# Splitting chains into single steps and ordering all steps anew, in a scan with a feed-forward block

## The chip, the cores and the metric

The kernel runs on one core of a Trainium2 chip. The metric is the device time of one execution in microseconds; the shown time is the median of three executions. A core has TensorE (PE in the profile, with its weight loads as PEld), VectorE (DVE), ScalarE (ACT), GpSimd (POOL) and SyncE (SP), whose queue issues the transfers of this kernel.

## The reference

Two blocks follow each other. The first is a scan with a state (4 batches, 8 heads, 768 tokens, head size 32, state size 16), the second a normalised feed-forward layer with a gate (3072 tokens, 256 features, 1536 hidden features), all in float32:

```python
log_a = np.log(np.clip(a, 1e-06, 1.0))
# per chunk of tokens, per batch and head:
cum = np.cumsum(la, axis=-1)
L = np.exp(cum[:, :, :, None] - cum[:, :, None, :]) * causal
y_intra = (C B^T * L) x
y_inter = C state * exp(cum)
state = exp(sum(la)) * state + sum_j B_j x_j exp(cum_last - cum_j)
# then, on (tokens, heads * head size):
xn = x / np.sqrt(np.mean(x * x, axis=-1, keepdims=True) + 1e-06) * rms_g
g = xn @ w_gate
out = (g * sigmoid(g) * (xn @ w_val)) @ w_out
```

The three weights arrive as 64-bit words and are turned into float32 on the chip.

## The kernel before

The 3072 tokens are worked through in six blocks of 512. A block has two pairs; a pair is two chunks of 128 tokens, in each of which the scan is computed in the two halves of 64. Per block the steps are:

- the scan: sums of logarithms and their exponentials `L` (ScalarE), products `g` of B and C (TensorE), their product with `L` (VectorE, L637 to L655), added states `A` (TensorE) and the running states `S` (VectorE, `states`, L685), the outputs `y` (TensorE, L709 and L740);
- the norm: `y` copied out into `yt` (`taken_out`, L805) and squared into `sq` (`squares`, L783), means by a product `ms` (L826), their root `rs` on ScalarE (`norm_roots`, L838), sent to memory and back, spread over the partitions, as `rb` (L849), then `xn` (L856);
- the gate and the value: for a pair of feature blocks `j`, seven products `P.1.j` to `P.7.j` of Strassen's scheme (`product_gv`, L947) in place of eight. A `take` copies a partial sum out of PSUM (ScalarE, L969), a `C` adds it to another (VectorE, L974), `silu` and `hid` follow;
- the output: twenty products `O.k` in two halves each (`product_o`, L1074) in place of twenty-seven, on sums of hidden values made by `u` and `up` (VectorE and GpSimd, L1058) and of weights. Totals `w.n` (`total_o`, L1097) bring them together on VectorE and ScalarE; `put` stores 128 rows. The product 1 uses the same part of PSUM as the product 11, so `O.1.0` waits until `w.18`, the total that reads product 11, has read it.

Block 0 starts before the weights are there. Its feature blocks 0 to 5 are made by plain products (`early.f.s` on values that are not yet normed, L883, and `gate.f`, L874), the other six by Strassen's scheme, and its output by a plain `o.f` (L996).

The startup goes like this. GpSimd builds masks: `never`, `after`, `hmask`, `upto` (L289, L298). VectorE casts `never` to `whole16`, and the steps `mask.p.h` write it with a product to the PSUM of a decay (L471). `idle.7` is seven products on zeros with no reader (L339). `a` is transposed (`aT`, L344), its logarithm `la0` taken, and products sum it: `r.0` (L400), `d`, `c` (L424 to L440). `parts.0` splits the sums in three 16-bit parts by four dependent operations on VectorE (L406), `turn` and `T` transpose B and C (L549, L565), `sums.p.h` (L478) adds the sums into the decays and `exp.p.h` (L500) takes the exponential.

A piece `k` of the weights goes through `fetch.k` (SyncE), `pow.k` (`power`, L217: three dependent operations on ScalarE), `man.k` (`mantissa`, L231: two on VectorE) and `wt.k` (L240: one on VectorE that joins both).

What sets the order: the kernel is built under a manual schedule, so every engine and SyncE's queue run their instructions in the order in which the program issues them. That order is a string `order` of 1667 steps (L1283), which a loop runs through (L1451). A step such as `0:gg.3/2` is the block, the kind, its numbers and the PSUM slot that it takes; `*2` behind a step puts two filler products into its bank first. The dictionaries `first_kinds` (L1199, block 0) and `kinds` (L1256) give the function for each kind. PSUM of block 0 has three slots of two banks (`/0`, `/1`, `/2`), given back by `switch.0` and `switch.1` to the tiles of the later blocks.

Of the kernel before, what the change touches and what calls it, by code (L numbers as in the profile page):

```python
# [10 lines left out]
I32 = mybir.dt.int32  # L11
# [9 lines left out]
def kernel(  # L21
# [195 lines left out]
    def power(k):  # L217
        words16, (lo, hi), dst, shape = fetched[k]
        n = shape[1] * shape[2]
        e = cvt.tile([P, n], FP32, tag="e", name="e", bufs=4)  # L220
# [6 lines left out]
        activation(out=b16, in_=g, func=AF.Prelu, scale=-2.0 ** 27, bias=kinks[:, 2:3],  # L227
                             alpha=2.0 ** -20)
        parts[k, "e"] = b16.bitcast(BF16)

    def mantissa(k):  # L231
        words16, (lo, hi), dst, shape = fetched[k]
        m = cvt.tile(shape, I32, tag="m", name="m")
        nc.vector.tensor_scalar(out=m, in0=hi, scalar1=0xFFFFF, scalar2=0x100000,  # L234
                                op0=ALU.bitwise_and, op1=ALU.bitwise_or)
        parts[k, "f"] = f = m.bitcast(FP32)
        nc.vector.scalar_tensor_tensor(out=f, in0=lo.bitcast(U32), scalar=2.0 ** -32, in1=m,  # L237
                                       op0=ALU.mult, op1=ALU.add)
# [54 lines left out]
    def whole_chunks():  # L293
        nc.vector.memset(chunk_ones, 0.0)
        for u, r in enumerate(halves):
            nc.vector.memset(chunk_ones[r, u], 1.0)
# [12 lines left out]
    def of_quarters():  # L309
        nc.vector.tensor_scalar(out=three, in0=part[:, 3:4], scalar1=-1.0, scalar2=1.0,  # L310
                                op0=ALU.mult, op1=ALU.add)
        nc.vector.tensor_scalar_add(later_part, part[:, 0:1], -1.0)
        nc.vector.tensor_scalar(out=third_part, in0=part[:, 2:3], scalar1=-1.0, scalar2=None,
                                op0=ALU.mult)
# [4 lines left out]
    def from_middle():  # L319
        nc.vector.tensor_copy(out=mid, in_=upto)  # L320
        nc.vector.tensor_scalar_add(mid[0:HC], mid[0:HC], -1.0)

    def from_middles():
        nc.gpsimd.tensor_copy(out=mid, in_=upto)
        for r in halves:
# [3 lines left out]
        minus_mid()  # L329

    def mask16():
        for r in halves:
            nc.vector.tensor_copy(out=never16[r], in_=never[r, r])

    def kinks_of_powers():
        for k, v in enumerate((1152.0 - 7.5 / 16, 256.0, -1792.0 * 128.0)):
            nc.vector.memset(kinks[:, k:k + 1], v)
# [68 lines left out]
    def three_parts(k):  # L406
        r_ps = ps.pop(("r", k))
        room = nrm.tile([P, 4, P], FP32, tag="lead1", name="room", bufs=1)
        first, second = [room[:, k].bitcast(BF16).rearrange("p (s m) -> p s m", s=2)
                         for k in range(2)]  # L410
        nc.vector.tensor_copy(out=first, in_=r_ps)
        rest = room[:, 2:4]
        nc.vector.scalar_tensor_tensor(out=rest, in0=first, scalar=later_part, in1=r_ps,
                                       op0=ALU.mult, op1=ALU.add)
        nc.vector.tensor_copy(out=second, in_=rest)
        rows[k] = row = const.tile([P, 2, P], BF16, name="row%d" % k)
        nc.vector.scalar_tensor_tensor(out=row, in0=second, scalar=third_part, in1=rest,
                                       op0=ALU.mult, op1=ALU.add)
# [31 lines left out]
    def chunk_decays():  # L450
        activation(out=full.rearrange("p g h -> p (g h)"), in_=ps.pop("c"), func=AF.Exp)
        nc.gpsimd.tensor_tensor(out=fsel, in0=full,
# [52 lines left out]
    def causal(L):  # L505
        for r in halves:
            nc.gpsimd.affine_select(out=L[r], in_=L[r], pattern=[[0, L.shape[1]], [1, HC]],  # L507
                                    compare_op=ALU.is_ge, fill=0.0, base=0, channel_multiplier=-1)

    def spread(g):  # L510
        b, c = divmod(g, NC)
        o = (c * BH + b * NH) * HC
        for u, r in enumerate(halves):
            nc.sync.dma_start(out=pair_tile(g)[r].rearrange("p h m -> p (h m)"),
                              in_=rowv[u, o:o + NH * HC].partition_broadcast(HC))
# [8 lines left out]
    def exponential(g):  # L524
        L = pair_tile(g)
        activation(out=L, in_=L, func=AF.Exp)
        causal(L)

    def decays(g):
        subtract(g)  # L530
        exponential(g)
# [153 lines left out]
    def states(p):  # L685
        A_ps = ps.pop(("A", p))
        b, c0, chunks = chunks_of(p)
        new = ssd.tile([P, 2, 2, 2, D], FP32, tag="A", name="A")
        for u in range(2):
            n = sum(v == u for i, v in chunks)  # L690
            if n:
                nc.vector.tensor_tensor(
                    out=new[:, u, 0:n], in0=A_ps[u][:, 0:n],
# [799 lines left out]
```

## Time and profile before

| | |
|---|---|
| time, median of 3 (lowest, highest) | 390.96 us (390.77, 391.19) |
| span of the profiled execution | 389.5 us |
| TensorE busy | 383.3 us, 98% |
| VectorE busy | 289.8 us, 74% |
| ScalarE busy | 226.4 us, 58% |
| GpSimd busy | 152.0 us, 39% |
| chain that ended last, on TensorE | 87% |

The profile holds one execution of its own; its span is from the first to the last record, and no separate device time is recorded for it, so it is set beside the median of the three runs. In a timeline each row is start, length, engine, line of the code, operation, output and inputs by the program's names, shape and number of instructions grouped; behind it, in brackets, an idle time of the engine and what ended it. In the view by stretches a row is the stretch, its length, and for each engine the busy time with the number of instructions, then the granted clock of TensorE, the share of the transfer engines and GB/s. In the waits a row is the engine and line that waited, what it waited for, the total, how often and the longest.

### The profile page before, as it was taken

Reading aid. Unit: us, or ns where it says so; the run is one execution under the profiler, and the core shown is the slowest. Engines: PE = TensorE matmul, PEld = TensorE weight load, DVE = VectorE, ACT = ScalarE, POOL = GpSimd, SP = SyncE. Lnnn points to the kernel's source line nnn. Section 1 sums busy time; section 2 is a strip of 40 time slices with the busy share of each in tenths; the row PEclk is TensorE's granted clock in tenths of the full one; section 3 lists DMA queues with packets and bytes.
Section 4 is the critical chain, followed back from the end, with each engine's and each line's share of the span. In section 5 each row is a group of like instructions: output and inputs, shape, how many; then the busy total and the mean of one; then the engine's idle time right before and its main releaser. Section 6 shows DMA issues by size and latency. Waiting matters only on the chain.

```text
span 389.5 us, 9637 instructions
## 1 busy us (share of the span) xinstructions
PE 383.3 (98%) x3805; PEld 329.8 (85%) x3805; DVE 289.8 (74%) x612; ACT 226.4 (58%) x471; POOL 152.0 (39%) x168
## 2 busy tenths in 40 slices
PE   8999999999999999999999999999999999999996
PEld 5676478788888999888899988899888899988995
DVE  6999999997976988669594765768374577454684
ACT  2899979988767262665865234763444571345420
POOL 5022045523693455343577701364611234212231
PEclk9999999999999999999999999999999999999999
DMA  8978984474073414634336112000100001000001
GB/s 107 241 153 259 240 195 147 120 157 42 3 101 86 50 13 94 145 42 96 70 78 81 27 42 42 2 15 22 56 3 2 2 12 50 29 0 0 2 0 56
DMA packets 109940, 28.05 MB, mean 72 GB/s; under 512 B 94824, under 2 KB 103752, under 8 KB 109896
## 3 DMA queue, kind: packets, MB, share of 16 engines
q1 hardware_dynamic: 107816, 27.31, 32.8%
q8 instruction: 30, 0.49, 0.5%
q10 hardware_dynamic: 2080, 0.13, 0.4%
q14 instruction: 14, 0.11, 0.1%
HBM read 23.69 MB, written 3.74 MB: 70 GB/s over the span
## 4 chain that ended last, share of the span: by engine, by line
PE 87%; DVE 9%; issue 2%; ACT 1%; DVEq 0%; ACTq 0%
PE gate L965 29%; PE o L1086 23%; PE val L965 21%; PE o L997 5%; PE y L750 3%; PE g L613 1%; DVE wgv L243 1%; DVE m L237 1%; DVE m L234 1%; DVE hid L912 1%; PE g L606 1%; PE e L474 1%; PE y L678 1%; DVE L L652 1%; ACT yt L821 0%
## 5 line engine op out<-in xcount | busy, mean ns | idle before, releaser
L977 DVE TENSOR_TENSOR c<-val,p 128x512 f32<-128x512 f32 x99 | 67.4, 686 | 45.1 <-PE val L965 33.3
L971 ACT COPY p<-gate 128x512 f32<-128x512 f32 x99 | 56.8, 581 | 57.5 <-PE gate L965 55.4
L965 PE MATMUL gate<-tx,wgv 128*128 128x256 f32 x264 | 65.9, 381 | 0.0
L215 ACT ACTIVATE c<-c 128x256 f32<-128x256 f32 x99 | 40.0, 415 | 38.7 <-DVE c L977 38.4
L990 POOL TENSOR_TENSOR hid<-c 128x256 f32<-128x256 f32 x31 | 24.7, 800 | 87.1 <-ACT c L215 83.1
L965 PEld LDWEIGHTS gate<-tx,wgv 128*128 128x128 f32 x264 | 49.2, 190 | 7.3 <-ACT p L971 0.7
L1117 DVE TENSOR_TENSOR ob<-ob,o 128x128 f32<-128x128 f32 (+1 forms) x90 | 24.2, 298 | 21.7 <-PE o L1086 16.9
L990 DVE TENSOR_TENSOR hid<-c 128x256 f32<-128x256 f32 x68 | 34.5, 521 | 6.9 <-ACT c L215 6.7
L1086 PE MATMUL o<-two,hid 128*128 128x128 f32 x280 | 36.5, 276 | 0.1
L1086 PEld LDWEIGHTS o<-two,hid 128*128 128x128 f32 x280 | 34.5, 192 | 1.1 <-DVE hid L990 0.4
L965 PE MATMUL val<-xn,wgv 128*128 128x256 f32 x132 | 33.7, 381 | 0.0
L965 PE MATMUL val<-tx,sw 128*128 128x256 f32 x132 | 33.5, 380 | 0.0
L965 PE MATMUL val<-xn,sw 128*128 128x256 f32 x132 | 33.3, 381 | 0.0
L965 PE MATMUL gate<-tx,sw 128*128 128x256 f32 x132 | 33.1, 381 | 0.0
L965 PE MATMUL gate<-xn,wgv 128*128 128x256 f32 x132 | 32.8, 381 | 0.0
L507 POOL TENSOR_SCALAR_AFFINE_SELECT L<-L 64x512 f32<-64x512 f32 x32 | 23.6, 737 | 18.6 <-ACT L L215 17.4
L965 PEld LDWEIGHTS val<-xn,wgv 128*128 128x128 f32 x132 | 24.8, 190 | 3.5
L965 PEld LDWEIGHTS val<-tx,sw 128*128 128x128 f32 x132 | 24.8, 190 | 3.5 <-issue 0.2
L965 PEld LDWEIGHTS gate<-tx,sw 128*128 128x128 f32 x132 | 24.7, 190 | 3.5 <-ACT p L971 0.2
L965 PEld LDWEIGHTS gate<-xn,wgv 128*128 128x128 f32 x132 | 24.3, 190 | 3.4 <-DVE hid L912 0.3
L965 PEld LDWEIGHTS val<-xn,sw 128*128 128x128 f32 x132 | 24.4, 190 | 3.2 <-issue 0.2
L215 ACT ACTIVATE e<-e,kinks 128x512 f32<-128x512 int16 (+1 forms) x36 | 26.0, 722 | 1.2
(203 smaller groups left out, 717.0 us busy)
## 6 DMA issues: line engine op xcount, KB each, us to landing
L<-rowd SPq DMA_DIRECT2D x32, 128.0 KB, 3.4
xr<-in_x_dram SPq DMA_DIRECT2D x24, 128.0 KB, 3.2
wr<-in_moe_w_out_dram SPq DMA_DIRECT2D x6, 512.0 KB, 5.6
out_dram<-ob SPq DMA_DIRECT2D x24, 128.0 KB, 1.8
wr<-in_moe_w_gate_dram SPq DMA_DIRECT2D x5, 512.0 KB, 5.8
wr<-in_moe_w_val_dram SPq DMA_DIRECT2D x5, 512.0 KB
br<-in_B_dram SPq DMA_DIRECT2D x23, 64.0 KB, 2.6
dT<-rowe SPq DMA_DIRECT2D x10, 128.0 KB
```

Of the source, the lines that this page charges most:

```text
L215: nc.scalar.activation(**operands)
L234: nc.vector.tensor_scalar(out=m, in0=hi, scalar1=0xFFFFF, scalar2=0x100000, op0=ALU.bitwise_and, op1=ALU.bitwise_or)
L237: nc.vector.scalar_tensor_tensor(out=f, in0=lo.bitcast(U32), scalar=2.0 ** -32, in1=m, op0=ALU.mult, op1=ALU.add)
L507: nc.gpsimd.affine_select(out=L[r], in_=L[r], pattern=[[0, L.shape[1]], [1, HC]], compare_op=ALU.is_ge, fill=0.0, base=0, channel_multipli ...
L750: nc.tensor.matmul(out=y[2 * k + u][rows, (2 * n + i) * HC:(2 * n + i + 1) * HC], start=(k, u, rows.start) not in opened, stop=True, skip_ ...
L965: nc.tensor.matmul(out=dst[:, half[w]], lhsT=lhsT, rhs=rhs, start=(k in (1, 2, 5) and w == 0), stop=True, skip_group_check=True)
L971: nc.scalar.copy(out=t, in_=Xs[j])
L977: nc.vector.tensor_tensor(out=t, in0=Zs[j], in1=a, op=ALU.add)
L990: engine.tensor_tensor(out=hid[:, 2 * j + c // 10 - 1, c % 10 - 1], in0=u, in1=src[:, half[1]], op=ALU.mult)
L997: nc.tensor.matmul(out=o, lhsT=hid[:, f, k // 2, (k % 2) * P:(k % 2 + 1) * P], rhs=wo[:, f], start=opens, stop=(f == NF - 1), skip_group_c ...
L1086: nc.tensor.matmul(out=Os[blk, b][:, place * P:(place + 1) * P], lhsT=hidden_or_sum(u)[:, g], rhs=rhs, start=(blk, b) not in opened, stop= ...
L1117: nc.vector.tensor_tensor(out=o, in0=o, in1=src, op=ALU.add if what[0] == "+" else ALU.subtract)
```

## The change

Functions that issued several instructions get a number more and issue one instruction per step: `power` (three steps), `mantissa` (two), `three_parts` (four), `squares`, `taken_out`, `states` (with `new_states` apart, now the kind `Sn`), `norm_roots` (three), `spread` (two transfers), `causal` (the two selections on GpSimd, now the kind `ca`, apart from the exponential `ex`), `put` for block 0 (copy `putc`, store `put`), and the small constants of the start. The operations are the same but for one: `xn.0`, one operation on 128x1024, becomes two on 128x512. The checks that a PSUM slot is free (`held`, `leave`) leave the program; they issued nothing.

The string `order` is written anew, with 1896 steps. The steps of TensorE are the same set, with `idle.7` and `c*2` as they were. Against the old order, the steps differ from the start up to the first products of block 1, and then in stretches: the second half of block 1's products and its output, the end of block 2, block 3, block 4, and the output of block 5. Between these stretches the order is unchanged.

```diff
-    def power(k):
+    def power(k, stage):
...
-        activation(out=k16, in_=words16, func=AF.Relu, scale=1.0 / 16, bias=kinks[:, 0:1])
-        activation(out=g, in_=k16, func=AF.Prelu, scale=-1.0, bias=kinks[:, 1:2],
-                             alpha=2.0 ** -20)
...
+        if stage == 0:
+            activation(out=k16, in_=words16, func=AF.Relu, scale=1.0 / 16, bias=kinks[:, 0:1])
+        elif stage == 1:
+            activation(out=g, in_=k16, func=AF.Prelu, scale=-1.0, bias=kinks[:, 1:2],
+                       alpha=2.0 ** -20)
...
-    def mantissa(k):
+    def mantissa(k, stage):
...
-    def three_parts(k):
+    def three_parts(k, stage):
...
+    def new_states(p, u):
...
-            nc.vector.tensor_tensor(out=xns[0], in0=yts[0],
-                                    in1=r.unsqueeze(1).to_broadcast([P, 2, TB]), op=ALU.mult)
+            nc.vector.tensor_tensor(out=xns[0][:, t], in0=yts[0][:, t], in1=r, op=ALU.mult)
...
     order = """
-        0:warm 0:a 0:set 0:bc.0 0:ident 0:bc.1 0:bc2.1.1 0:ones 0:zeros 0:ident16 0:whole 0:kinks
-        0:idle.7 0:gcol 0:x.0 0:never 0:after 0:fetch.0 0:fetch.1 0:x.1 0:whole16 0:mask.0.0/0
-        0:part 0:hmask 0:upto 0:mid 0:mids 0:part2 0:aT 0:mask.1.1/2 0:la0 0:log4.0.4 0:upto2 0:r.0
-        0:fetch.2 0:head 0:sel 0:middles 0:after2 0:fetch.3 0:log4.4.2 0:log4.6.2 0:bc.3 0:tmask
-        0:parts.0 0:log 0:c*2 0:cx 0:mask.0.1/1 0:turn.0 0:Tb.0 0:T.0 0:d 0:dx 0:sums.0.1 0:sums.0.0
-        0:exp.0.1 0:never16 1:exps 0:exp.0.0 0:turn.1 0:scale.1.0 0:scale.1.1 0:last.1 0:cc
...
-        0:P.2.3 0:bc.4 0:x.4 0:switch.0 0:pow.11 0:P.1.3 0:P.1.4 0:take.1.3 0:C.11.3 0:P.2.4 0:P.6.3
-        0:yt.2 0:sq.2 0:gg.3/2 0:take.1.4 0:silug.11.3 0:C.11.4 0:L.3.0 0:take.6.3 0:cwp.3.3 0:P.5.3
-        0:cwp.1.0 0:P.7.3 0:silug.11.4 0:P.6.4 0:take.7.3 0:P.5.4 0:P.4.3 0:hidgp.11.3 0:wt.11
...
-        0:spread.8 0:ms.1 0:take.6.5 0:P.7.5 0:rs.1 0:pow.13 0:sub.9 0:o.0/2 0:o.1 0:sub.10 0:man.13
...
+        0:warm 0:a 0:set 0:bc.0 0:ident 0:bc.1 0:bc2.1.1 0:ones 0:zeros 0:ident16 0:whole.0 0:head
+        0:kinks.1 0:part 0:whole.2 0:part2.0 0:after 0:hmask 0:upto 0:never 0:mid.0 0:mid.1
+        0:whole16 0:part2.2 0:part2.1 0:mask.0.0/0 0:eps 0:never16.0 0:x.1 0:aT 0:fetch.0 0:mids
+        0:gcol 0:x.0 0:fetch.2 0:fetch.1 0:idle.7 0:kinks.2 0:upto2 0:whole.1 0:after2 0:la0
+        0:log4.0.4 0:log4.4.2 0:log 0:r.0 0:middles.0 0:tmask 0:parts.0.0 0:parts.0.1 0:parts.0.2
+        0:d 0:dx 0:sel 0:parts.0.3 0:scale.1.1 0:c*2 0:cx 0:middles.2 0:middles.1 0:ch 0:turn.0
+        0:sums.0.0 0:log4.6.2 0:exp.0.0 0:turn.1 0:mask.1.1/2 0:sums.1.1 0:scale.0.1 0:T.0 0:Tb.0
...
+        0:A.0 0:kinks.0 0:bc.2 0:rowout.1 0:pow.0.0 0:pow.0.1 0:fetch.5 0:L.0.1 0:tok 1:exps
+        0:Sn.0.1 0:S.0.0 0:g.1.0/2 0:g.1.1/0 0:L.1.0 0:S.0.1 0:L.1.1 0:y.0/1 0:r.1 0:parts.1.0
+        0:tokout 0:pow.2.0 0:sq.0.0 0:pow.0.2 0:pow.2.1 0:A.1 0:Sn.1.1 0:parts.1.1 0:S.1.0 0:y.1/2
+        0:sq.0.1 0:pow.1.0 0:row.0 0:pow.1.1 0:sq.1.0 0:pow.3.0 0:pow.3.1 0:yt.0.0 0:wt.0 0:sq.1.1
+        0:mean 0:yt.0.1 0:early.0.0/0 0:yt.1.1 0:yt.1.0 0:rowe.0 0:pow.1.2 0:ms.0 0:rs.0.0 0:pow.3.2
...
+        0:switch.0 0:scale.5 0:S.3.3 0:silu.1 0:pow.11.0 0:pow.11.1 0:pow.11.2 0:P.1.3 0:yt.2.1
+        0:yt.2.0 0:take.1.3 0:P.1.4 0:P.2.3 0:take.1.4 0:sq.2.0 0:P.6.3 0:yt.2.2 0:sq.2.1 0:sq.2.2
+        0:take.6.3 0:yt.2.3 0:sq.2.3 0:man.11.1 0:P.2.4 0:C.11.4 0:C.11.3 0:wt.11 0:cwp.1.0
+        0:cwp.4.3 0:P.7.3 0:gg.3/2 0:L1.3.3 0:L.3.0 0:fetch.10 0:man.10.0 0:silug.11.3 0:pow.10.0
...
+        0:P.5.5 0:ms.1 0:rs.1.0 0:cwp.5.2 0:P.7.5 0:rs.1.1 0:o.0/2 0:spread.9.0 0:rs.1.2
+        0:spread.10.0 0:rb.1 0:take.7.5 0:P.4.5 0:o.1 0:pow.13.1 0:pow.13.2 0:man.13.1 0:C.22.5
+        0:wt.13 0:silug.21.5 0:o.2 1:cwp.2.0 0:sub.9 0:cw.0.2 0:hidgp.22.3 0:cwp.5.3 0:P.3.5
+        0:sub.10 0:pow.14.0 0:man.14.0 0:pow.15.0 0:pow.14.1 0:pow.14.2 0:cw.1.1 0:cw.0.1 0:cwp.0.3
+        0:man.14.1 0:wt.14 0:yt.3.0 0:xn.1.0 0:C.12.5 0:pow.15.1 0:pow.17.0 0:o.3 0:o.4 1:P.1.1
...
-        5:w.8 5:w.16 5:O.5.0 5:w.13 5:w.7 5:O.5.1 5:up.8 5:u.12 5:w.20 5:O.12.0 5:O.7.0 5:O.7.1
-        5:up.13 5:w.14 5:w.9 5:O.12.1 5:w.17 5:w.18 5:w.15 5:put.3 5:u.14 5:O.1.0 5:O.1.1 5:w.19
-        5:put.0 5:O.14.0 5:u.15 5:w.22 5:O.14.1 5:O.19.0 5:O.19.1 5:w.21 5:w.23 5:put.1 5:O.10.0
-        5:O.10.1 5:w.24 5:w.25 5:put.2
...
+        5:O.11.0 5:O.11.1 5:w.11 5:w.20 5:w.13 5:w.18 5:O.7.1 5:O.5.1 5:up.13 5:w.14 5:w.9 5:w.15
+        5:w.8 5:w.17 5:put.3 5:O.12.0 5:O.12.1 5:u.14 5:u.15 5:put.0 5:O.1.0 5:O.1.1 5:O.14.0
+        5:O.19.0 5:O.19.1 5:w.19 5:w.22 5:w.24 5:w.23 5:O.10.0 5:put.1 5:O.10.1 5:w.25 5:O.14.1
+        5:w.21 5:put.2
```

More of the change, by code (lines that the diff above doesn't have):

```diff
@@ L1253, in of_chunk @@
     def of_chunk(n, fn):
-        return when(n, lambda b, g: fn(4 * b + g))
+        return when(n, lambda b, g, *args: fn(4 * b + g, *args))
     kinds = {
@@ new lines @@
+        0:parts.1.3 0:man.3.1 0:fetch.4 0:dT.2 0:dT.3 0:sums.3 0:sums.2 0:exp.3 0:Tt.3.0 0:fetch.8
+        0:fetch.7 0:man.1.1 0:wt.1 0:wt.3 0:xn.0.0 0:exp.2 0:Tt.3.1 0:rowout.0 0:fetch.6 0:scale.2
+        0:x.2 0:man.2.0 0:xn.0.1 0:man.2.1 0:txp.0.0 0:txp.0.1 0:early.0.1 0:norm.0.0 0:tx.0.2
+        0:norm.0.1 0:man.5.0 0:silu.0 0:pow.2.2 0:wt.2 0:cw.0.0 0:turn.2 0:early.1.0/1 0:Tt.2.1
+        0:early.1.1 0:norm.1.0 0:pow.5.0 0:T.3 0:T.2 0:norm.1.1 0:man.4.0 0:Td.2 0:Td.3 0:S.1.1
+        0:pow.4.0 0:man.5.1 0:hid.0 0:man.4.1 0:pow.4.1 0:table.1 0:gate.2/0 0:Tt.2.0 0:gg.2/1
```

604 lines of the change are left out of this document (320 added, 284 removed).

## The prediction, made before the changed kernel was run

> **What bounds the kernel now.** I read the page first (busy shares, then the chain that ended last), then the busy time by stretches, the waits of TensorE, and only then the timelines of the stretches that are not full.
>
> ```profile
> span 389.5 us, 9637 instructions
> ...
> PE 383.3 (98%) x3805; PEld 329.8 (85%) x3805; DVE 289.8 (74%) x612; ACT 226.4 (58%) x471; POOL 152.0 (39%) x168
> ...
> PE 87%; DVE 9%; issue 2%; ACT 1%; DVEq 0%; ACTq 0%
> ```
> ```profile
> 0.00:10.00 10.00, 8.76 (x51) 5.73 (x53) 6.61 (x31) 3.06 (x7) 5.01 (x17) 1.00 0.86 114
> 10.00:20.00 10.00, 9.35 (x172) 6.38 (x172) 9.35 (x20) 8.70 (x16) 0.00 (x0) 1.00 0.92 225
> ...
> 360.00:380.00 20.00, 20.00 (x149) 19.03 (x148) 14.45 (x28) 6.35 (x19) 6.33 (x6) 1.00 0.00 1
> ```
> ```profile
> PE y L719 <- DVE S L700: 0.5, 1, 0.5
> PE g L613 <- ACT sq L215: 0.5, 1, 0.5
> PE o L1086 <- DVE ob L1117: 0.4, 1, 0.4
> ```
>
> TensorE is busy for 383.3 of 389.5 us, and the chain lies on it for 87%. The stretch 360 to 380 us shows 20.00 of 20.00, with VectorE at 14.45. The new order issues the same TensorE steps, each as often as before. So only three things can move the end: the startup before TensorE is full (the first 21 us), the few waits after it (`g` 0.5, `o` 0.4), and new waits that the new order makes. The program whose span is 389.5 us stands 1.5 us under the median of the runs, 390.96; I make the sum on the span and add it to the median.
>
> **The startup.** These rows carry it (start, length, engine, line):
>
> ```profile
> 1.11 1.67 PE L342 MATMUL idle<-warm 128*128 128x256 bf16 x7 [1.11 <-DVE warm L368]
> ...
> 1.40 0.36 POOL L290 TENSOR_SCALAR_AFFINE_SELECT never<-never 128x128 f32<-128x128 f32 x1
> ...
> 2.37 0.29 POOL L290 TENSOR_SCALAR_AFFINE_SELECT upto<-ones 128x128 f32<-128x128 f32 x1
> ...
> 2.41 0.33 DVE L384 CAST whole<-never 128x128 bf16<-128x128 f32 x1
> ...
> 2.79 1.01 PE L474 MATMUL e<-whole,ident 128*128 128x512 bf16 x2
> ...
> 2.86 0.21 DVE L320 COPY mids<-upto 128x128 f32<-128x128 f32 x1
> ...
> 3.60 0.52 PE L347 MATMUL aT<-ident,a_sb 96*128 96x96 f32 x2
> ...
> 5.09 1.19 PE L402 MATMUL r_ps<-mids,early_ones 128*128 128x256 f32 x2
> ...
> 7.62 0.60 PE L474 MATMUL e<-whole,ident 128*128 128x512 bf16 x2
> ...
> 10.13 1.94 ACT L215 ACTIVATE L<-e 128x1024 f32<-128x1024 f32 x2
> ...
> 16.18 2.35 DVE L652 TENSOR_TENSOR L<-g,L 128x1024 f32<-128x1024 f32 x2
> ...
> 19.51 0.61 DVE L702 SCALAR_TENSOR_TENSOR S<-S,fcol,A 128x64 f32<-128x64 f32 x2
> ...
> 20.72 0.45 PE L719 MATMUL y<-T,S 32*64 32x128 f32 x8
> 21.10 0.49 PE L1161 MATMUL r_ps<-mids,la 128*128 128x128 f32 x2
> ...
> 22.08 0.59 PE L402 MATMUL r_ps<-mids,early_ones 128*128 128x256 f32 x2
> 22.51 3.62 PE L889 MATMUL gate<-yt,wgv 128*128 128x256 f32 x16
> ...
> 33.04 3.60 PE L879 MATMUL gate<-xn,wgv 128*128 128x512 f32 x8
> ```
>
> In the new order POOL makes `never` last, behind `upto`. By the 0.36 and 0.29 of the two it is ready at about 2.65 instead of 1.76, and VectorE puts the two `mid` steps (0.21 for the like) ahead of the cast. The mask, which opened at 2.79, opens at about 3.25, and it is now TensorE's first work, because `idle.7` is moved behind `aT`. The transposed `aT` follows 0.81 later, at 4.1. Then the seven idle products stand between `aT` and `r.0`. Before, they filled an empty stretch (1.11 to 2.78) at no cost; now I charge 1.5, of which about 0.7 is covered by the logarithm that `r.0` needs anyway. `r.0` starts at about 5.9 against 5.09: +0.8.
>
> Between `r.0` and the first exponential there were 5.0 us (5.09 to 10.13), with a mask and a sum over chunks in it that are now placed later; `d` and `c` replace them ahead of `turn.0` and `sums.0.0`. With the parts of the rows on VectorE in between, I get 4.7, and the first exponential at 10.6, 0.5 late. The bounds are 9.9 and 11.9: the two masks of the same form start 0.81 apart at 2.79 (from it to `aT`) and last 0.60 at 7.62, so the same product costs about twice as much early on as late, and I cannot see from one trace whether that change waits for time or for work done.
>
> From there ScalarE is dense: four exponentials (1.94 for two) and the copies between, the last ending at about 16.9. VectorE then has the four products with `L` at 1.18 each (2.35 for two) and the states; `S.1` waits for `L.1.0` on VectorE, so the last `L` ends at about 20.5 and `y.1` at about 22.2, where it ended at 21.17. That is +1.0. But `r.1` (22.08 to 22.51, 0.43) is already done in the new order, since it is placed ahead of `y.1`. The lag that TensorE carries into the first `early` products is +0.6, and I take +0.7 with the wait for `yt`. From there to `gate.2` TensorE has the same work. Bounds: -0.6 with an early exponential, +1.9 with a late one.
>
> Whether the lag is taken back depends on VectorE, which in 10 to 20 us is busy 9.35 of 10.00, as TensorE is. Here the splitting of the chains acts: `man` in two, `pow` in three, `parts` in four, with other work between.
>
> ```profile
> 24.52 0.69 DVE L237 SCALAR_TENSOR_TENSOR m<-wr,m 128x512 f32<-128x512 uint32 x1
> 25.13 0.42 DVE L539 TENSOR_TENSOR Bd<-br,d_sb 128x256 f32<-128x256 f32 x1
> ...
> 28.77 0.69 DVE L237 SCALAR_TENSOR_TENSOR m<-wr,m 128x512 f32<-128x512 uint32 x1
> 29.56 0.69 DVE L243 SCALAR_TENSOR_TENSOR wgv<-m,e 128x512 f32<-128x512 f32 x1
> ```
>
> Behind the same operation an independent one starts after 0.61, a dependent one after 0.79. So a link of a chain that gets other work behind it gives VectorE back 0.18. The six `man` and the six links of `parts` ahead of `gate.2` make 2.2 us of VectorE, and that is why I let VectorE hold TensorE's lag and not add to it. It is no gain in the sum, as TensorE has no wait there to give back but the lag. The Trainium skill, "VectorE: DVE Perf Modes", section "The DRAIN you can't avoid", says that the flush of the pipe follows every operation whether chained or not, and that a semaphore behind each of eight copies cost nothing extra. By that rule the split gives VectorE nothing, and the startup would be +0.7 plus up to those 2.2 us; the 0.79 beside 0.61 of this trace speaks against it.
>
> The clock has a rule as well. The Trainium skill, "TensorE: Matmul & The Clock Gate", section "Part 1: The HAM clock gate", says that the array runs at half rate until a free-running window of about 3.4 us was busy, and that it is time and not a count of products that warms it. The mask at 0.81 and then 0.43 to 0.60 agrees in kind, while the page's granted clock shows 1.00 in both stretches. By that rule a first product at 3.25 instead of 1.11 makes TensorE warm between about 6.7 and 10.1 us, which is rival A at its far end.
>
> **The wait of `gg.3`.** One step of TensorE after another, up to `g`:
>
> ```profile
> 53.30 1.03 PE L965 MATMUL val<-xn,wgv 128*128 128x256 f32 x4
> 54.16 1.03 PE L965 MATMUL gate<-tx,sw 128*128 128x256 f32 x4
> 55.70 0.70 PE L613 MATMUL g<-T 32*64 32x128 f32 x32 [0.50 <-ACT sq L215]
> ```
>
> A step of four products takes 0.86 (53.30 to 54.16), so the next could have started at 55.02; it started at 55.70: 0.68 lost, waiting for the squares of `y.2`. In the new order six P steps stand ahead of `gg.3` instead of five (0.86 more cover), and the squares are mixed with the copies. But `P.7.3`, one of the six, needs `take.6.3`, which is now behind the squares on ScalarE, by my walk 0.3 late. Net -0.4, between -0.7 and +0.2. Beside it `ms.1` and `P.7.5`: `take.6.5` has more ahead of it on ScalarE: +0.1 (-0.1 to +0.3).
>
> **Transfers.** The roots of block 0's second half go through memory:
>
> ```profile
> sq<-roots SPq DMA_DIRECT2D x20, 64.0 KB, 3.0
> ```
> ```profile
> 74.20 1.95 SPq L852 DMA_DIRECT2D sq<-roots  x4
> ```
> ```profile
> 81.51 1.40 DVE L861 SCALAR_TENSOR_TENSOR xn<-yt,gcol,sq 128x512 f32<-128x512 f32 x2
> ```
>
> The last of the four issues ends at 76.15, lands 3.0 later (the median of the DMA issues), at 79.2, and `xn` starts at 81.51: 2.3 to spare. In the new order fewer transfers stand between the roots and their return on SyncE's queue (one, where a fetch and two were), worth about 0.9, but TensorE has eight steps between `ms.1` and `1:P.1.1` where it had nine, 0.86 less. So I find 2 us of slack and charge 0; if that cover is gone, block 1 starts late by what is missing. Fetches of weights move by less than a microsecond each against their conversion: 0.
>
> **The tail.**
>
> ```profile
> 381.52 0.61 PE L1086 MATMUL o<-two,hid 128*128 128x128 f32 x4
> ...
> 382.51 1.16 PE L1086 MATMUL o<-sw,hid 128*128 128x128 f32 x8 [0.38 <-DVE ob L1117]
> ...
> 384.40 1.06 PE L1086 MATMUL o<-two,hid 128*128 128x128 f32 x8
> ...
> 385.30 1.06 PE L1086 MATMUL o<-wo,hid 128*128 128x128 f32 x8
> ```
>
> Eight of these take 0.90 (384.40 to 385.30), four 0.45; 381.52 + 0.45 leaves 0.54 idle before `O.1.0`, which waits for the total `w.18`. In the new order `w.18` stands behind `O.11`, and `O.7.1`, `O.5.1` and `O.12` (four halves, 1.8 us) lie between it and `O.1.0`. The wait goes; next late would be `u.15`, with 0.4 to spare. I take -0.6, with what little else stands open there (-0.7 to 0). What follows the last product is the same: one total, one store.
>
> **The other stretches** (blocks 1 to 4, locally in another order). TensorE is full there, so there is hardly a gain; one new wait of the listed size would cost 0.4 to 0.5. I take +0.2, between -0.3 and +1.0 (two new waits).
>
> **Sum:** +0.7 - 0.4 + 0.1 - 0.6 + 0.2 = 0.0 on a span of 389.5, so 390.9 against the median of 390.96.
>
> **Rivals.** A, slower: TensorE warms up late. `r`, `d`, `c` and `turn` then run at the early rate, the first exponential comes at 11.9 and the startup term is +1.9: 392.1. It decides when the first exponential starts after 11.2. For it speaks that the first product is over 2 us later; against it that the idle products keep TensorE busy from 3.25 on. B, slower: a new wait in the full part, the return of the roots to `xn` or `P.7.3` behind the squares, 1 to 2 us each: 391.9 to 392.9. It decides when a wait over 1 us stands behind 21 us. C, faster: the startup does not lag (first exponential at 10.2 or before, and the 0.18 of each link taken back by VectorE), while the two waits go: 390.96 - 0.4 - 0.6 = 390.0, down to 389.3 with the startup at -0.6. D: the split does nothing because TensorE is the bound; that is part of my forecast.
>
> **Chances.** About 0.2% (0.8 us) is what a measurement of this kernel can tell from no change. Forecast, within 0.8 us of 390.96: 0.36. A 0.21 and B 0.13, both slower: 0.34. C 0.30. The range 389.2 to 392.7 leaves out the far ends of B and of C with a second gain, together under 2 in 10; the forecast's own is 390.2 to 391.7.
>
> **What would show it.** The first mask at about 3.25 and `r.0` at 5.9; the first exponential between 10.2 and 11.2; the end of `y.1` near 22.2; the first `gate` product of 512 columns 0.7 later than 33.04; `g` no longer among the waits and `o` gone from the tail. I am wrong if the first exponential is outside these bounds, or if TensorE shows a new wait of over 0.5 us between 60 and 360 us.

## The result, and the profile after

The changed kernel takes 395.24 us (median of 6 runs, 395.09 to 396.84), the kernel before 390.91 beside it: 1.0113 times as long, with an interval of 1.0093 to 1.0133. I had forecast 390.9 and a range up to 392.7. The page of the changed kernel, its span, busy times and chain:

```profile
span 393.2 us, 9649 instructions
...
PE 384.3 (98%) x3805; PEld 327.9 (83%) x3805; DVE 287.6 (73%) x613; ACT 224.8 (57%) x471; POOL 149.8 (38%) x168
...
PE 84%; DVE 8%; ACT 6%; issue 1%; POOL 0%; ACTq 0%; POOLq 0%; DVEq 0%
```

TensorE still has 3805 products, the same ones, and is busy for 1.0 us more; the span is 3.7 us longer. The waits of TensorE (what waited, for what, total, times, longest):

```profile
PE e L501 <- DVE whole L401: 3.3, 1, 3.3
PE gate L1002 <- DVE ob L1154: 0.7, 1, 0.7
PE o L1123 <- DVE ob L1154: 0.6, 1, 0.6
PE gate L1002 <- ACT p L1008: 0.4, 1, 0.4
PE gate L914 <- DVE wgv L252: 0.3, 1, 0.3
```

The waits of `y`, `g` and the last `o` are gone. In their place stand 0.7 and 0.6 on totals (`ob`), and these are not in the startup or the tail but in stretches where TensorE was full before. The view by stretches (TensorE's busy time stands behind the length):

```profile
10.00:20.00 10.00, 10.00 (x140) 6.22 (x138) 7.53 (x15) 7.96 (x14) 1.62 (x2) 1.00 0.94 217
...
205.00:215.00 10.00, 9.31 (x73) 8.06 (x57) 8.00 (x14) 4.94 (x11) 6.90 (x8) 1.00 0.61 77
258.00:268.00 10.00, 9.38 (x81) 8.49 (x80) 6.86 (x13) 4.86 (x14) 5.38 (x4) 1.00 0.07 22
```

The last two answer to these of the kernel before, in which TensorE was full:

```profile
203.00:213.00 10.00, 10.00 (x70) 9.41 (x69) 5.51 (x15) 6.35 (x12) 6.90 (x8) 1.00 0.72 102
254.00:264.00 10.00, 10.00 (x88) 9.47 (x87) 6.90 (x14) 5.31 (x15) 5.43 (x4) 1.00 0.10 28
```

Between 10 and 20 us the roles are swapped: TensorE is now full (10.00, before 9.35) and VectorE is not (7.53, before 9.35).

Since the products are the same, the time lost can be followed along the trace. I take the start of the n-th product in both traces, at those n where both kernels have issued the same set of products, and subtract. This lag of the changed kernel is:

| at (us, before) | lag (us) | what lies ahead of it |
|---|---|---|
| 33 (`gate.2`) | 2.0 | startup |
| 56 (behind `gg.3`) | 1.0 | the wait of `gg.3` is gone, and smaller ones |
| 76 to 134 | 1.25 | `ms.1` and the weights' last pieces |
| 161 | 2.0 | end of block 1 |
| 206 | 2.1 | |
| 219 | 3.2 | end of block 2 |
| 269 | 4.35 | block 3 |
| 381.5 | 4.3 | |
| 382.5 (`O.1.0`) | 3.7 | the tail's wait is gone |

Each trace is one execution. What a trace brings out of the startup varies by about 1 us between executions of kernels with the same startup; the steps of 1.1 in block 2 and in block 3 come again, within 0.02, in every later trace that keeps the new order there.

The rows of the startup on TensorE that answer to those of before:

```profile
3.34 1.01 PE L501 MATMUL e<-whole,ident 128*128 128x512 bf16 x2 [3.34 <-DVE whole L401]
...
5.96 0.98 PE L419 MATMUL r_ps<-mids,early_ones 128*128 128x256 f32 x2
...
15.69 1.13 PE L628 MATMUL g<-T 32*128 32x256 f32 x8
...
22.61 0.45 PE L746 MATMUL y<-T,S 32*64 32x128 f32 x8
...
23.60 1.99 PE L926 MATMUL gate<-yt,wgv 128*128 128x256 f32 x8
```

The first mask (3.34) and `r.0` (5.96) are where I had put them. From the first mask on TensorE has hardly a break, and still it is 1.1 late at the first `early` product (23.60 against 22.51).

### The profile page after: what moved, and what is told of

It reads as the page before. It is cut to its first block, busy times and chain, and to the rows that moved or that the text cites. A ratio compares the mean times of both kernels' runs of the same rounds, so it can differ in the third digit from the quotient of the medians.

```text
span 393.2 us, 9649 instructions
## 1 busy us (share of the span) xinstructions
PE 384.3 (98%) x3805; PEld 327.9 (83%) x3805; DVE 287.6 (73%) x613; ACT 224.8 (57%) x471; POOL 149.8 (38%) x168
## 4 chain that ended last, share of the span: by engine, by line
PE 84%; DVE 8%; ACT 6%; issue 1%; POOL 0%; ACTq 0%; POOLq 0%; DVEq 0%
PE gate L1002 27%; PE val L1002 20%; PE o L1123 20%; PE o L1034 5%; PE gate L914 4%; PE y L777 2%; PE g L635 1%; ACT e L215 1%; DVE c L1014 1%; DVE hid L1027 1%; ACT p L1008 1%; DVE tx L979 1%; PE g L628 1%; DVE ob L1154 1%; ACT u L215 1%
## 5 line engine op out<-in xcount | busy, mean ns | idle before, releaser
L1027 POOL TENSOR_TENSOR hid<-c 128x256 f32<-128x256 f32 x31 | 23.4, 756 | 85.9 <-ACT c L215 82.0
L1027 DVE TENSOR_TENSOR hid<-c 128x256 f32<-128x256 f32 x68 | 31.7, 481 | 12.6 <-ACT c L215 12.3
```

The costliest lines, as they stand in the source:

```text
L1027: engine.tensor_tensor(out=hid[:, 2 * j + c // 10 - 1, c % 10 - 1], in0=u, in1=src[:, half[1]], op=ALU.mult)
```

## The experiments

All kernels are made of the new functions and an order of steps. Where both orders have issued the same set of steps, they can be cut and joined. With each group of runs the kernel before was measured again: 391.15 with e1 to e4, 391.05 with e5 to e8, 390.80 with e9 to e12, 391.14 with e13 to e15. A ratio is to that.

**The splitting alone, and the three parts of the order.**

```diff
 e1: the old order, each chain spelled out in its place
-0:pow.0 0:wt.0 ... 0:parts.0 ... 1:sq ...
+0:pow.0.0 0:pow.0.1 0:pow.0.2 0:wt.0 ... 0:parts.0.0 0:parts.0.1 0:parts.0.2 0:parts.0.3 ... 1:sq.0 1:sq.1 1:sq.2 1:sq.3 ...
 e2: as e1, but the new order from the start to the first product of block 1
 e3: as e1, but the new order in the re-planned stretches of blocks 1 to 4
 e4: as e1, but the new order for the output of block 5
```

> The new functions with single steps, but every step put where its chain stood in the order of before, so that only `xn.0` in two pieces differs in what is issued. Theory 1 (the time is lost by the places of the steps, not by the splitting): 390.9, within 0.4 us of before. Rival (single steps cost something by themselves, for instance the two pieces of `xn.0`): slower by 0.5 us or more.

> The new order up to the first product of block 1, the order of before from there. Theory 1 (each re-planned stretch adds its own lag, and TensorE, being full behind it, gives nothing back): the lag of 1.25 us that the changed kernel's trace shows at 80 us stays to the end, so 392.1 to 392.4. Rival (the lag of the startup is taken back by waits that the order of before has later, or grows): 390.9 or under, or above 393.

> The order of before up to block 1's products and for the output of block 5, the new order in the five re-planned stretches of blocks 1 to 4 between. Theory 1: the lag that the changed kernel gains between 80 and 370 us, 4.45 - 1.25 = 3.2 us, comes without the new startup as well: 393.9 to 394.4. Rival (the middle loses only because the startup was late and work runs into each other): under 392.5.

> The order of before with only the output of block 5 in the new order. Theory 1: the two waits of TensorE at 380 to 382 us go, as in the changed kernel, where the lag falls from 4.46 to 3.73: 390.2 to 390.4, faster than before by 0.5 to 0.7. Rival (the gain belongs to the lag before it, which gave VectorE and GpSimd time): 390.8 or more.

Measured, beside 391.15 for before: e1 390.69 (ratio 0.9994, 0.9984 to 1.0004), e2 392.86 (1.0048, 1.0036 to 1.0061), e3 394.45 (1.0095, 1.0081 to 1.0109), e4 390.29 (0.9977, 0.9965 to 0.9989). So the splitting alone changes nothing that can be measured. The startup, with what `gg.3` gives back, costs 1.7, a little more than expected; the middle 3.3; the tail gives back 0.9, of which its trace shows 0.55 at the tail. The sum, 4.1, is near the whole 4.3. But e2, e3 and e4 are made of e1's functions, and counted from e1's 390.69 the parts are 2.2, 3.8 and -0.4, 5.5 in all against 4.6 for the whole, so they add up only to within about 1 us. In e3 the lag grows from -0.55 at 134 us to 2.65 at 381, by 3.2, in the same three places as in the changed kernel, without its startup.

**Why the full stretches wait: block 2.** VectorE, GpSimd and TensorE of the changed kernel, in this order:

```profile
208.68 0.48 DVE L1154 TENSOR_TENSOR ob<-ob,o 128x128 f32<-128x128 f32 x2
209.07 2.74 DVE L979 TENSOR_TENSOR tx<-xn,tx 128x256 f32<-128x256 f32 x1
211.74 0.47 DVE L1154 TENSOR_TENSOR ob<-ob,o 128x128 f32<-128x128 f32 x2
```
```profile
208.96 0.65 POOL L534 TENSOR_SCALAR_AFFINE_SELECT L<-L 64x512 f32<-64x512 f32 x1 [2.75 <-ACT L L215]
209.59 0.72 POOL L1027 TENSOR_TENSOR hid<-c 128x256 f32<-128x256 f32 x1
210.27 1.26 POOL L1097 TENSOR_TENSOR s<-s,hid 128x512 f32<-128x512 f32 x1
211.61 1.34 POOL L1097 TENSOR_TENSOR hid<-hid 128x512 f32<-128x512 f32 x1
```
```profile
213.75 1.13 PE L1002 MATMUL gate<-xn,wgv 128*128 128x256 f32 x4 [0.69 <-DVE ob L1154]
```

`tx.3` reads two operands in SBUF and takes 2.74 us instead of 0.42. It ends at 211.81, just behind the first break in the row of GpSimd's operations (211.53 to 211.61), and lasts 2.74 in all seven traces that have this row. The totals behind it come late, and TensorE waits for them.

```diff
-2:ex.0 2:ca.0.0 2:w.1 2:hidp.12.4 2:up.6 2:up.7 3:C.11.0 2:tx.2 2:O.4.1 ... 2:w.6 2:tx.3 2:O.18.0
+2:ex.0 2:ca.0.0 2:w.1 2:hidp.12.4 2:up.6 2:up.7 3:C.11.0 2:tx.2 2:tx.3 2:O.4.1 ... 2:w.6 2:O.18.0
```

> The changed kernel with one step of VectorE, `2:tx.3`, moved up behind `2:tx.2`. In the changed kernel it starts at 209.07 beside a row of GpSimd operations without a gap (208.96 to 212.95) and lasts 2.74 us instead of 0.42. Theory 1 (an operation of VectorE on two operands of SBUF is held while GpSimd works, and the totals behind it release PSUM late): started before 208.96 it lasts 0.4, and the wait of `3:P.1.1` (0.86 of lag at 212 us) goes down to 0.2 or less. Rival (the wait comes from the place of the totals themselves behind `u.10`, and the long record is only a late end): the lag at 220 us stays at 3.2 within 0.2, less any other start.

On VectorE, with this step right behind `tx.2`, ahead of GpSimd's row:

```profile
209.34 0.42 DVE L979 TENSOR_TENSOR tx<-xn,tx 128x256 f32<-128x256 f32 x1
209.68 0.48 DVE L1154 TENSOR_TENSOR ob<-ob,o 128x128 f32<-128x128 f32 x2
```

The operation lasts 0.42, and the wait of `3:P.1.1` is gone. A wait of 0.25 came up earlier at an `O`, so the lag against the changed kernel falls by 0.62 over this place (from +0.66 to +0.04), not by the whole 0.86. Theory 1 holds here, by the trace. The median is 394.94 (ratio 1.0093, 1.0062 to 1.0124); beside the changed kernel's 1.0113 (1.0093 to 1.0133) the time alone would not show the gain.

**The same in block 3.** VectorE, GpSimd and TensorE of the changed kernel:

```profile
258.61 0.68 DVE L1014 TENSOR_TENSOR c<-val,p 128x512 f32<-128x512 f32 x1
259.83 1.50 DVE L1027 TENSOR_TENSOR hid<-c 128x256 f32<-128x256 f32 x1 [0.54 <-ACT c L215]
261.26 0.68 DVE L1014 TENSOR_TENSOR c<-val,p 128x512 f32<-128x512 f32 x1
```
```profile
259.78 1.27 POOL L1097 TENSOR_TENSOR hid<-hid 128x512 f32<-128x512 f32 x1
```
```profile
264.99 1.16 PE L1123 MATMUL o<-wo,hid 128*128 128x128 f32 x8 [0.62 <-DVE ob L1154]
```

```diff
-3:silu.12.2 3:hid.12.2 3:O.3.0 3:O.3.1 3:w.4 3:yt.0 3:P.3.5 3:C.12.5 3:up.1
+3:silu.12.2 3:O.3.0 3:O.3.1 3:w.4 3:yt.0 3:P.3.5 3:C.12.5 3:hid.12.2 3:up.1
```

> The changed kernel with `3:hid.12.2` moved down behind `3:C.12.5` on VectorE. In the changed kernel it starts at 259.83 beside a GpSimd operation, lasts 1.50 instead of 0.41, and `C.12.5`, `silu.12.5`, the loading of a table and the copy that `O.6.1`'s followers wait for are queued behind it. Theory 1: `C.12.5`, which reads PSUM, starts at about 260.1 instead of 261.26, and the wait of TensorE at 264 us (0.85 of lag) goes down to 0.2 or less. Rival (the wait belongs to the table that ScalarE loads for the norm, which stands ahead of the copies in either order): the 0.85 stays within 0.2.

```profile
258.32 0.68 DVE L1014 TENSOR_TENSOR c<-val,p 128x512 f32<-128x512 f32 x1
259.93 0.69 DVE L1014 TENSOR_TENSOR c<-val,p 128x512 f32<-128x512 f32 x1 [0.93 <-PE val L1002]
```

`C.12.5` starts at 259.93, the loading of the table on ScalarE and the copy behind it move with it, and the lag over this place falls by 0.95: the whole wait is gone. The table was not the cause. The median is 394.86 (ratio 1.0084, 1.0054 to 1.0113), again too near the changed kernel's to show the gain without the trace; the two moves together are in e10.

**One place in a queue, in the startup.** Two steps that stand behind another engine's wait in the changed kernel, each moved up alone:

```diff
 e7
-0:silu.0 0:pow.2.2 0:wt.2
+0:exp.2 0:pow.2.2 ... 0:man.2.1 0:wt.2 ... 0:silu.0
 e8
-0:sums.1.0 0:last.1 0:Tl.1 0:rowe.1 0:exp.1.0
+0:sums.1.0 0:exp.1.0 0:last.1 0:Tl.1 0:rowe.1
```

> The changed kernel with the last link of a chain, `0:pow.2.2`, moved up behind `0:exp.2` on ScalarE, and `0:wt.2` behind `0:man.2.1` on VectorE. In the changed kernel `pow.2.2` waits at 33.48 behind `silu.0`, and `gate.2` waits 0.44 for `wt.2`. Theory 1 (the split let the last link slip behind a wait of another chain): the gap of 0.44 ahead of `gate.2` goes. Rival (the product is bound by TensorE's own work there, and another wait comes in its place): the lag at `gate.2` against before stays within 0.15.

> The changed kernel with `0:exp.1.0` moved up behind `0:sums.1.0` on ScalarE, ahead of `Tl.1` and `rowe.1`. In the changed kernel ScalarE waits 0.96 ahead of `Tl.1`, though the sums are ready at 15.3, and the exponential starts at 16.23; then `g.1.0`, which takes its PSUM, comes at 17.6 and the last two products with `L` on VectorE at 18.88 and 20.22. Theory 1 (one place in ScalarE's order costs the startup): the exponential starts at about 15.4, `y.1` ends 0.5 to 0.8 earlier, and so does the first `early` product. Rival (VectorE's order bounds it, with `rowout.1` waiting for the same bank): less than 0.2.

Theory 1 fails in both. The medians are 395.87 and 395.86 (ratios 1.0113 and 1.0117, the changed kernel's is 1.0113), and the lag against the changed kernel does not go down over either place. What came in instead of the wait for the weight, in e7:

```profile
PE gate L914 <- DVE hid L936: 0.3, 1, 0.3
```

`gate.2` now waits as long for `norm.0.1` to leave its PSUM slot. In e8 `rowout.1` on VectorE waits 1.07 for `rowe.1`, which the exponential pushed back, and the next product with `L` stands behind it. Links were late, but each was one of several that were late together.

**When the products get short.** In the profiles of these kernels the startup's first products take about twice as long as later ones, and the moment at which this ends differs between kernels and executions. I read it from each trace as the start of the first product that takes its later time:

| first product at | kernels | first short product at | first exponential at |
|---|---|---|---|
| 1.1 | before, e1, e3, e4, e11, e13, e14 | 5.7 to 7.4 | 9.4 to 10.2 |
| 3.3 | changed, e2, e5 to e8 | 6.4 to 9.3 | 10.05 to 11.1 |

So the later first product makes the short products 1.6 and the first exponential 0.9 later on the average, and either kind varies by about 1 us in the exponential. The view by stretches shows a granted clock of 1.00 in all of them. But the record of the clock that each trace holds has its first entry, full clock, only at 5.65 to 7.24 us in the traces of the first row and at 6.39 to 9.27 in those of the second, so the 1.00 ahead of it is no reading, and where the record begins it agrees with the products. The first exponential goes with this moment: from 10.05 at 6.39 (e6) to 11.14 at 9.27 (e7). At the same moment, 6.74 and 6.77, the changed kernel's comes 0.3 later than that of e14 (10.22 against 9.94), so of the 0.9 about 0.6 goes with the clock. To undo the late start:

```diff
-0:whole.0 0:head 0:kinks.1 ... 0:upto 0:never 0:mid.0 0:mid.1 0:whole16 ... 0:fetch.1 0:idle.7 0:kinks.2
+0:whole.0 0:idle.7 0:never 0:whole16 0:head 0:kinks.1 ... 0:upto 0:mid.0 0:mid.1 ... 0:fetch.1 0:kinks.2
 e10: also
+0:mask.1.1/2 0:r.0 (the mask stood behind 0:turn.1), 2:tx.3 as in e5, 3:hid.12.2 as in e6
```

> The changed kernel with `idle.7` back ahead of the first mask and `never` and `whole16` back ahead of the other small constants, as in the order of before; nothing else moved. Theory 3 (in the new order TensorE is full from the first mask on, so that the 2.2 us by which its first product is later are lost but for what it can catch up while the logarithm is awaited): the first product is at 1.1 again, `r.0` at 5.1 instead of 5.96, and the lag behind that falls by 0.7 to 0.9 and stays gone: 394.4 to 394.6. Rival (the place of the idle products costs nothing, because VectorE and ScalarE bound the stretch to 24 us): the lag at `gate.2` is as in the changed kernel within 0.2, beside runs with the same time of the first exponential.

> The moves of the run before, `mask.1.1` moved back ahead of `r.0`, and the two moves of VectorE's steps, `2:tx.3` and `3:hid.12.2`, together. Theory 3: the mask then fills the wait for the logarithm and takes 0.5 more out of TensorE's full stretch; theory 1: the moves in blocks 2 and 3 take out 0.6 and 0.95 beside it. Sum 0.8 + 0.5 + 0.6 + 0.95 = 2.85, so 392.3 to 392.8. Rival (gains of the startup are swallowed by the next wait, as it was with the weight and with the exponential): 393.5 or more.

e9 was a miss: 395.35, no gain. Its rows on TensorE show why:

```profile
3.42 0.53 PE L364 MATMUL aT<-ident,a_sb 96*128 96x96 f32 x2
5.00 1.19 PE L419 MATMUL r_ps<-mids,early_ones 128*128 128x256 f32 x2 [1.04 <-POOL mids L381]
```
```profile
11.20 1.02 ACT L215 ACTIVATE L<-e 128x1024 f32<-128x1024 f32 x1 [0.58 <-PE e L522]
```

`r.0` came 0.96 earlier, as expected, but TensorE now had a break of 1.04 ahead of it, and its products stayed long until about 10.3 (the clock record begins at 10.26; 11.25, which stands in the expectation of e15, is the start of the first transposing product of the later length). Its first exponential is the latest of all, though that of e7 (11.14) is near. In e10, with the mask in that break, they were short from 6.3, the exponential came at 9.46, and the lag at 58 us was 0.4 where the changed kernel has 1.2. Its time, 393.01 (ratio 1.0054, 1.0041 to 1.0067), is 2.2 under the changed kernel, somewhat less than the 2.45 to 2.95 that I had expected. Whether the break or the mask's work made the difference was told apart by:

```diff
 e15: as e9, and
-0:aT 0:fetch.0
+0:aT 0:idle.5 0:fetch.0
```

> The kernel of the run with the idle products moved back, with five more idle products behind `aT`, where TensorE had nothing to do for 1.3 us. They compute nothing. Theory 5 (the products get short once TensorE has been busy without a break for some microseconds): short products from about 6 to 7.4 us instead of 11.25, the first exponential at 9.4 to 10.2 instead of 11.2, and the time 0.8 to 1.2 under that run: 394.2 to 394.6. Rival (the short products come at a time of their own, or the gap costs by itself): first exponential over 10.5, time within 0.4 of that run.

```profile
3.43 0.52 PE L364 MATMUL aT<-ident,a_sb 96*128 96x96 f32 x2
3.75 1.27 PE L359 MATMUL idle<-warm 128*128 128x256 bf16 x5
5.04 1.00 PE L419 MATMUL r_ps<-mids,early_ones 128*128 128x256 f32 x2
```
```profile
9.31 1.02 ACT L215 ACTIVATE L<-e 128x1024 f32<-128x1024 f32 x1 [0.35 <-PE e L522]
```

`r.0` starts at the same time as in e9 within 0.04, but the products are short from 5.87 instead of 10.3 (clock record from 5.72 instead of 10.26), and the time is 394.36 (ratio 1.0071, 1.0050 to 1.0092, against 1.0111, 1.0095 to 1.0127, of e9), 1.0 less. Five products that compute nothing are worth about a microsecond here, because they leave no break. Each of the two kernels was traced once, and e9's trace is of the slowest of its four runs (394.09 to 395.87), so the 1.9 between the exponentials is more than the medians differ. The Trainium skill, "TensorE: Matmul & The Clock Gate", section "Part 1: The HAM clock gate", gives a mechanism: half rate until at least one free-running window of about 3.4 us was busy. By my estimate from that figure this is one to two windows, 3.4 to 6.8 us, from the first product. The traces have 3.0 to 6.0 us from the late first product, 4.6 to 6.3 from the early one, and 5.3 from the end of the break in e9, which agrees but for the shortest, 3.0.

**The two costs by themselves.** A kernel that measures them alone, in one execution.

> No part of the reference is computed; four copies of each of five kinds of VectorE operations on 128x256 run with GpSimd idle, and then beside a row of GpSimd additions of 128x512 without a gap; behind them TensorE's products on 32 rows, two row groups apart from the other two, and all four together. Theory 1: VectorE's addition of two operands in SBUF takes 0.4 alone and is held for whole GpSimd operations (1.27 us each) beside them, the one with an operand in PSUM is not held. Rival (the long records are late ends and not held operations): both stay within 0.1. For TensorE, theory 3: the two halves together take about as long as one alone (1.1 for 16 records and for 8); rival: twice as long.

On VectorE, four operations in each row; "free" with GpSimd idle but for one addition from 2.01 to 3.27, "held" beside a row of them:

```profile
2.57 2.00 DVE L32 TENSOR_TENSOR twofree<-src 128x256 f32<-128x256 f32 x4
4.48 1.41 DVE L34 TENSOR_TENSOR psumfree<-psum,src 128x256 f32<-128x256 f32 x4
5.81 0.89 DVE L36 TENSOR_SCALAR onefree<-src 128x256 f32<-128x256 f32 x4
...
8.96 1.42 DVE L32 TENSOR_TENSOR twoheld<-src 128x256 f32<-128x256 f32 x4
...
16.77 1.41 DVE L34 TENSOR_TENSOR psumheld<-psum,src 128x256 f32<-128x256 f32 x4
...
23.48 3.58 DVE L36 TENSOR_SCALAR oneheld<-src 128x256 f32<-128x256 f32 x4
```
```profile
2.01 1.26 POOL L26 TENSOR_TENSOR big<-src 128x512 f32<-128x512 f32 x1 [1.57 <-DVE src L22]
9.11 1.84 POOL L51 TENSOR_TENSOR big<-marktwo,src 128x256 f32<-128x256 f32 x1 [5.84 <-DVE marktwo L50]
```

Operations with an operand in PSUM take 1.41 in both. Those with one operand in SBUF go from 0.89 to 3.58, which I had not expected. The additions of two SBUF operands were not held beside the row: they had started first, and then it was GpSimd's operation that took 1.84 instead of about 0.72. They were held in the row called free, by the one addition there (2.00). So both places of the expectation came out the other way round, and the reason is the order of the starts: who starts first goes through, and the other waits. This is what the Trainium skill says in "SBUF — State Buffer", section "Who interferes with whom": VectorE and GpSimd share a pair of ports, which whoever issues first has for the whole instruction, and an instruction of VectorE with at most one input in SBUF is outside of it unless it runs in a mode that uses both of VectorE's ports. The traces agree on who is held. They show one thing more: `tx.3` with its 2.74 is held through three GpSimd operations in a row. That is the exception. The operations with one operand in SBUF are held here for one GpSimd operation each, though that row has no break either. What lets an operation in between two of GpSimd's was not taken apart.

On TensorE:

```profile
14.42 1.13 PE L69 MATMUL g<-src 32*128 32x256 f32 x8
15.48 1.13 PE L62 MATMUL full<-src 128*128 128x256 f32 x4
...
18.67 1.16 PE L69 MATMUL g<-src 32*128 32x256 f32 x16
19.76 1.99 PE L62 MATMUL full<-src 128*128 128x256 f32 x8
```

Two row groups alone (8 records) take from 14.42 to 15.48, 1.06; all four (16 records) from 18.67 to 19.76, 1.09. Halves of `g` that stand apart cost as much each as both together. In the startup of the changed kernel the half at 15.69 stands alone, as does each half of the added states.

**A better kernel?**

```diff
 e11: as e4, and
-0:P.6.3 0:yt.2.0 ... 0:sq.2.3 0:gg.3/2 0:take.1.4 ... 0:cwp.3.3 0:P.5.3
+0:P.6.3 0:yt.2.0 ... 0:sq.2.3 0:P.5.3 0:gg.3/2 0:take.1.4 ... 0:cwp.3.3
 e13: as e4, and from switch.1 to 1:table, where both orders have issued the same steps, the relative order of the new kernel
 e14: the same from gate.2 to the first product of block 1
```

> The order of before with the output of block 5 in the new order, and one step moved in block 0: `P.5.3` ahead of `gg.3`, so that a step of 0.86 covers the 0.67 that `gg.3` waits for the squares. Theory: the wait goes, 0.5 to 0.65 faster than with the tail alone (390.29): 389.6 to 389.9. Rival (the wait only moves, since `L.3.0` and `P.7.3` behind it come later): 390.2 or more.

> The order of before up to `switch.1`, then what is left of block 0's first stretch in the relative order of the new one (the stretch with `gg.3`), then the order of before again, and the output of block 5 in the new order. Theory 4 (the new order gains at `gg.3` by the copies and squares mixed, whatever the startup was): the wait of 0.67 ahead of `gg.3` goes without another in its place, 0.4 to 0.9 faster than with the tail alone: 389.4 to 389.9. Rival (the gain needs the later startup, as VectorE and ScalarE had more time there): 390.2 or more.

> The same with the cut at `gate.2`, so that the new order holds from 33 us to the first product of block 1, and the output of block 5 in the new order. Theory 4: besides `gg.3` it takes the small gains between 37 and 50 us (0.4) and the loss at `ms.1` (0.3 to 0.4): within 0.3 of the run before. Rival (the new order's stretch lives on weights that its own startup had prepared earlier, so that weights come late in it): slower than the run before by 0.5 or more.

All three missed: 390.85 (ratio 1.0004, 0.9995 to 1.0012), 391.61 (1.0015, 0.9998 to 1.0032) and 391.77 (1.0009, 0.9992 to 1.0027), none better than e4's 390.29. TensorE in e11, and in e13:

```profile
56.13 1.10 PE L1002 MATMUL val<-tx,sw 128*128 128x256 f32 x4 [0.86 <-DVE c L1014]
```
```profile
51.16 1.99 PE L1002 MATMUL gate<-xn,wgv 128*128 128x256 f32 x8 [0.91 <-DVE hid L949]
```

The step that was to cover the wait of `gg.3` has a wait of its own, 0.86 for `C.11.3`; and the new order's stretch behind the old startup waits 0.91 for a `hid`. In e14 TensorE waits 0.8 for a transposed `T` and 0.4 for a weight. Between `gate.2` and 58 us the new order's steps lose 1.1 in e13 and 0.9 in e14, where behind their own startup they gain 0.8, also in e10, whose lag at `gate.2` is 0.75 smaller than that of the changed kernel. So the gain at `gg.3` belongs to the new order as a whole; which of the things that the new startup has ready makes it was not tested. Of all kernels here e4 is the fastest: the old order with the new tail.

## Why the prediction was wrong, point by point

- **"So only three things can move the end"** held, but its third item, new waits, was sized by the waits that the old order had. The step that failed is "The other stretches: +0.2, between -0.3 and +1.0 (two new waits)". It measured 3.2 (lag in e3) and 3.3 (time). Even with the upper bounds of all terms together, +3.4, the sum would have been 394.4. I let TensorE's fullness stand for slack in the engines around it. The order of VectorE's steps against GpSimd's decided half of it: moving two held operations took out 0.62 and 0.95 of lag (e5, e6, and e10 with both). I had walked these stretches for dependences and PSUM, and not for which operations of the two engines would run at the same time. What block 1 lost (0.75), and the rest of the 3.2, I did not take apart. A held operation by itself is not yet a loss: behind 20 us the trace of before has 15 operations of VectorE that last over 0.5 us longer than the shortest of their kind, each beside GpSimd's work, 11 us in all, and TensorE waits there only at `gg.3` and in the tail; the changed kernel has 21, 17 us in all. The two that cost TensorE time stand ahead of totals that it waits for.
- **The startup, +0.7** at `gate.2` (-0.6 to +1.9), measured 2.0 there in the changed kernel and 2.5 in e2 (1.9 to 3.0 in the six traces with the late first product), at and beyond its upper bound. The rows were right up to `r.0` (5.96 for 5.9), and the first exponential, 10.05 to 11.1, holds my 10.6. What failed stands behind it. I had called ScalarE dense from there; in the changed kernel it waits 0.40 and 0.96 between the four exponentials, and `y.1` ends at 23.06 for my 22.2, though the first exponential, 10.22, is earlier than forecast. And VectorE's chain did not set the lag, nor has TensorE "the same work": the same products, from 12.1 to 33 us of before, take 1.0 longer in the changed kernel, e2, e5 and e10 alike (21.9 for 20.9), although two waits of before are gone. Parts of it are halves standing apart (`g` 1.74 to 2.15, added states 0.52 to 0.72, start to start), the wait for `wt.2`, 0.44, the transposes (1.20 to 1.39) and `r.1` (0.43 to 0.63); against these 1.4 the wait of `y` is gone. Why the last two take longer in their new places was not tested.
- **Rival A** was partly right. The later first product does make the short products later, by 1.6 us on the average, and that costs 0.9 at the first exponential; but it did not come to the 11.9 that I gave it, and in the changed order it stayed under my 11.2. Against it I wrote that the idle products keep TensorE busy from 3.25 on. That is what they are worth: with a break in their place (e9) the clock record begins at 10.26, later than in all six traces with the late first product, and the exponential came at 11.20. The granted clock of 1.00, which I noted there for the first stretches, was no reading for the first microseconds.
- **Rivals B, C and D.** B had the right kind: new waits in the full part. They came on totals (0.69 and 0.62) and not on the roots or `P.7.3`, and neither reaches the 1 us by which B was to be told. My sign of being wrong, a new wait of over 0.5 us between 60 and 360 us, came twice. C did not come. D, that the split by itself does nothing, is what e1 shows.
- **`gg.3`, -0.4**: too small. The lag falls by 0.8 to 1.0 between 33 and 58 us, the wait of 0.68 with smaller ones, but only behind the new startup (e13, e14). **`ms.1`, +0.1**: right on balance; 0.4 of lag comes there, over my 0.3, and 0.3 goes again.
- **The tail, -0.6**: 0.55 of lag (4.28 to 3.73); 0.9 of time in e4 against before, 0.4 against e1. Right.
- **Transfers, 0**: no wait of TensorE in the changed kernel is for one. Right.
- **The 0.18 per link** had no part in the sum, and e1 shows that the split by itself has none. No run here takes a link alone out of its chain, so it stays open whether VectorE gains by it, and with it whether the 0.79 beside 0.61 of the trace means what I took it for.

## What to carry to other kernels

When a planner moves steps about a full engine, price the stretches by the engines around it: write VectorE's and GpSimd's operations side by side, and look for every operation with its operands in SBUF that falls beside a row of GpSimd work without a break and ahead of something that TensorE waits for. The same products are not the same time on TensorE: products of different row groups belong next to each other (1.09 for both halves together, 1.06 for each apart). And products that compute nothing can be worth what they cost when they fill a break in the first microseconds (1.0 us in e15 against e9).

## What the runs showed of the hardware that I had not expected

A VectorE operation can be held through several GpSimd operations (2.74 for 0.42, through three, in seven traces); the operations of e12 were held through one each. An operation with one operand in SBUF is held, and an addition with an operand in PSUM is not (0.89 to 3.58 for four, against 1.41 and 1.41). A break of 1.0 us in TensorE's first products put off their short time by over 4 us (about 10.3 against 5.87, one trace each).
